# Value tiles turned by transposes, with the router's logit columns made apart, in a fused attention and mixture-of-experts kernel

## The chip, the cores and the metric

The kernel is one program on one core of a Trainium2 chip. The metric is the time of one execution in microseconds (us); "before" is the median of three runs, 772.24 us (772.15 to 772.66). The engines named below are TensorE (PE, its weight loads PEld), VectorE (DVE), ScalarE (ACT), GpSimd (POOL) and the DMA queue of SyncE (SP).

## The reference

```python
B, H, S, D = 8, 8, 576, 64                      # q, k, v: (B, H, S, D), s: (B, H, S)
scores = scale * q @ k.T + minimum(-(cum_i - cum_j), 0), causal
attn   = softmax(scores)
x      = (attn @ v) as (B*S, H*D)               # 4608 rows of 512
logits = (x / |x|) @ (emb / |emb|).T / tau      # 8 experts
e      = argmax(logits);  g = softmax(logits)[e]
out    = g * (relu(x @ w1[e]) @ w2[e])          # w1: 512 x 1024, w2: 1024 x 512
```

Since x is a product with v, a row's logits are too: with E the normed embeddings of a head (64 x 8), logits = sum over heads of attn @ (v E), up to the norm. The kernel makes v E once, as extra columns of v, and reads the logits off the attention's output.

## The kernel before

**Steps.** The attention runs in 64 steps, one for each head n of each batch (n = 8b + c8, c8 = 0 to 7); `step(n)` writes out by hand what each engine does, and each engine works its instructions off in that order. A step makes head n's scores, key-major, as two PSUM tiles (`ta_`, `tb_`, `tbl`), takes their exponentials on ACT (`expa`, `expb1`), and on POOL the part of them that bf16 loses (`pl_`, tile PL). It makes the row maxima of head n+5 from a second set of products (tiles s, spare columns of ta; PE `s1`, `sa`, `s3`, `sb`; DVE `sr`, `s3`, `sbr`), and multiplies head n-2's probabilities with its values (`pv`, 45 matmuls into om), which DVE norms into the rows xt (`norm1` to `norm3` of head n-3). The s tiles have two buffers: the third product of a step needs the first one's maximum to be read, and the fourth the second's.

**Values.** v lies head-major in memory: `vTs[b % 2]` holds for a pair of heads p (64 dimensions each on 128 partitions) 640 key columns in float32. `emm(n)` turns two or three blocks of 128 keys in step n: the block is the stationary operand, the moving one is `EN[0][:, p]`, 128 x 144: 8 logit columns of the first head, the 128 columns of the identity, 8 logit columns of the second. The result V (128 keys x 144, bank m of PSUM, which has one buffer) is scaled and split in two float16 tiles, `vh` by ACT and `vl` by DVE (`vcp`). A batch has 20 such products in its eight steps: three in even steps, two in odd ones. `loadt` and `vsq`, in steps c8 = 0 to 5, load the next batch's v and take its squares for the scale `sc` (`vscale`, c8 = 6); the vT tile of a batch is dead once its last `emm` is done.

**Rest of a batch.** When a batch's eight heads are done, the router chooses experts and scatters the rows xt to DRAM, as small DVE, PE and POOL steps between those of the next batch (`slots`, `scatter`). After step 63 the experts' matrix products follow, from about 345 us to the end.

Of the kernel before, what the change touches and what calls it, by code (L numbers as in the profile page):

```python
# [42 lines left out]
CAP = 640  # L43
# [4 lines left out]
LAST = 3  # L48
OMW = 384
XSH = 4  # L50


def fused(tc, qkh, qkc, vtin, s_in, emb, tau, w1h, w2h, out, nb=B):
# [57 lines left out]
def main(ctx, tc, qkh, qkc, vtin, s_in, emb, tau, w1h, w2h, out, shared, nb):  # L111
# [16 lines left out]
    vjunk = const.tile([128, CAP], BF16, name="vjunk")  # L128
    P32J = vjunk[:, 0:S]
    junk = const.tile([128, 1024], BF16, name="junk")  # L130
    ones = const.tile([128, 128], F32, name="ones")
    identb, tri, onesb = (const.tile([128, 128], BF16, name=n) for n in ("identb", "tri", "onesb"))
    trim = const.tile([128, 320], BF16, name="trim")
    trib = trim[:, 64:192]
# [63 lines left out]
    def heat(k):  # L198
        for _ in range(k):
            nc.tensor.matmul(om, PLs[2][:, 512:640], PLs[2][:, 0:512], start=True, stop=True)  # L200
# [74 lines left out]

    def vscale(b):
        pb = om[:, 496:500]
        nc.tensor.matmul(pb, ones, VB[b]["sq"], start=True, stop=True)
        sc = p2.tile([128, 1], F32, name="sc", bufs=3)
        si = sc.bitcast(I32)  # L280
        ws = p2.tile([128, 2], F32, name="ws", bufs=3)
        first.append(partial(nc.vector.tensor_reduce, sc, pb, AX.X, ALU.add))
        first.append(partial(soon, partial(nc.vector.tensor_scalar, sc, sc, 1.0e-30, 1.0e30, op0=ALU.max, op1=ALU.min),
                             partial(nc.vector.tensor_scalar, si, si, -0.5, float((127 + 14) * (1 << 23) + (125 << 22)), op0=ALU.mult, op1=ALU.add),
                             partial(nc.vector.tensor_single_scalar, si, si, 0x7F800000, op=ALU.bitwise_and), partial(VB[b].update, sc=sc, ws=ws),
                             partial(nc.vector.tensor_scalar, ws[:, 0:1], sc, 1.0e-6 * 2.0 ** -XSH, None, op0=ALU.mult),
                             partial(nc.vector.tensor_scalar, ws[:, 1:2].bitcast(I32), si, -1.0, float((254 + XSH) << 23), op0=ALU.mult, op1=ALU.add)))

    def emm(n):
        b, p, js = n // H, n % H // 2, ((0, 1, 2), (3, 4))[n % 2]  # L290
        t = ps_m.tile([128, 512], F32, tag="m", name="V")
        for i, j in enumerate(js):
            nc.tensor.matmul(t[:, 144 * i:144 * i + 144], vTs[b % 2][:, p, 128 * j:128 * j + 128], EN[0][:, p], start=True, stop=True)
        VB[b]["V"] = t[:, 0:144 * len(js)].rearrange("p (j c) -> p j c", c=144)

    def vcp(n, low):
        b, p, j = n // H, n % H // 2, slice(3 * (n % 2), 3 + 2 * (n % 2))
        v = VB[b]
        if "vl" not in v:
            v["vl"] = p2.tile([128, 5, H // 2, 144], F16, name="vl")  # L300
        h = v["vh"][:, j, p, 1:145]
        if not low:
            return nc.scalar.activation(h, v["V"], AF.Copy, scale=v["sc"])
        nc.vector.scalar_tensor_tensor(v["vl"][:, j, p], v["V"], v["sc"], h, op0=ALU.mult, op1=ALU.subtract)  # L304

    def hset(g):
        if g < NGg:
# [26 lines left out]
    def prep(n, k):  # L334
        g, c = n // HG, n % HG
        if n < 0:
            return
        if g == 0:
            if c == 0:
                neg(1, False, 1 - k)  # L340
            elif c < 3:
                hcopy(1, k, c - 1)
            if c < 3:
                return
        if c == 3:
            neg(g + 2, k, 0)
        elif c == 0:
            neg(g + 1, k, 1)
        else:
            hcopy(g + 1, k, c - 1)  # L350
# [136 lines left out]
    def expa(n):  # L487
        P32 = HD[n]["P32"] = P32s[n % 3]
        nc.scalar.activation(P32[:, 0:576], HD[n]["ta"][:, 256:832], AF.Exp, scale=0.125)  # L489
# [61 lines left out]
    def rsetup():  # L551
# [4 lines left out]
        def r0():  # L556
            nc.scalar.activation(P32J[0:NE, 0:DM], em, AF.Square, accum_out=a)
            nc.scalar.activation(c, a, AF.Ln, bias=tiny[0:NE])
            nc.scalar.activation(b, c, AF.Exp, scale=0.5)
# [13 lines left out]
        def r8():  # L573
            pt = ps_m.tile([128, 512], F32, tag="m", name="pe")
            for k in range(4):
                nc.tensor.transpose(out=pt[:, NE * k:NE * k + NE], in_=em[:, 128 * k:128 * k + 128], identity=ident[0:NE, 0:NE])
            pt = pt[:, 0:4 * NE].rearrange("p (c e) -> p c e", c=4)
            for i in range(2):
                v.tensor_copy(en4[64 * i:64 * i + 64, :, 136 * i:136 * i + 8], pt[64 * i:64 * i + 64])
        r0()  # L580
        r7s.append(r8)
        for f in (r1, partial(v.reciprocal, c, b), partial(v.tensor_mul, c, c, a), partial(v.tensor_add, b, b, c),
                  partial(v.tensor_scalar, b, b, 0.5, 1.0e-6, op0=ALU.mult, op1=ALU.add), partial(v.reciprocal, c, b), r7):
            f()
# [407 lines left out]
    def step(n):  # L992
# [53 lines left out]
        (sa if n > 1 else s2)(m)  # L1046
        if n < 0:
            heat(1)
        if live:
            expa(n)  # L1050
            if n != 1:
                prep(n, True)
        norm3(n - 3)
        if n == NH + 1:
            nc.sync.dma_start(zero[0:1, 0:1], XT[nb - 1][0:1, 0, 432:433])
            HT["cap"] = 24
# [92 lines left out]
            vscale(b1)  # L1149
        if live and c8 < 4:  # L1150
            loadt(b1, c8)
        if n == NH - 8:
            wissue(3)
        for _ in range(SCN[c8] if n < NH - 22 else 1 + (c8 > 5) + 4 * (n > NH - 6) if n < NH - 2 else 5 * (n >= NH)):
# [328 lines left out]
```

## Time and profile before

| | us |
|---|---|
| median of 3 runs | 772.24 |
| profiled execution | 770.33 |
| its span, first to last instruction | 768.3 |
| PE busy | 743.2 |
| ACT busy | 570.8 |
| DVE busy | 525.1 |
| POOL busy | 383.5 |

The profiled execution is 1.9 us below the median of the runs, and its span is 2.0 us shorter than its own time. PE's busy time takes a matmul as busy until its results are written; matmuls follow one another faster than that, so what one costs in a stream is read from the distance of their starts.

### The profile page before, as it was taken

What the parts mean: (1) busy time and instruction counts of PE and PEld (TensorE: products, weight loads), DVE (VectorE), ACT (ScalarE), POOL (GpSimd) and SP (SyncE); (2) the same over time, 40 slices, a digit from 0 to 9 for tenths busy, and PEclk for the clock granted to TensorE, in tenths of its full rate; (3) what the DMA queues carried; (4) which work ended last, traced back from release to release, by engine and by line L of the source; (5) the groups of instructions that cost most, each with busy time, mean ns of one, the idle gap of its engine ahead of it and who ended that gap; (6) DMA issues with size and microseconds to landing.
All of it is one profiled execution on the core that took longest, in us unless ns stands there. A gap on an engine that the chain in (4) does not pass through costs nothing. (4 is left out here: it accounts for less than half of the span.)

```text
span 768.3 us, 22128 instructions
## 1 busy us (share of the span) xinstructions
PE 743.2 (97%) x8587; PEld 550.2 (72%) x8587; DVE 525.1 (68%) x1794; ACT 570.8 (74%) x1024; POOL 383.5 (50%) x371
## 2 busy tenths in 40 slices
PE   7799999999999999999899999999999999999996
PEld 3599999999999999997464545645655555555564
DVE  7677888888888888889567666655665567645621
ACT  7789999999999999988676877738548578474410
POOL 8957798989899898774622130131221302211002
PEclk9889999999999999999999999999999999999999
DMA  8977879797979798854645965654665756643001
GB/s 157 228 175 146 173 181 206 175 216 167 211 170 214 168 206 176 209 168 156 196 150 178 185 192 168 153 194 112 166 199 114 191 168 174 210 106 88 15 15 57
DMA packets 76965, 125.46 MB, mean 163 GB/s; under 512 B 38981, under 2 KB 39385, under 8 KB 75986
## 3 DMA queue, kind: packets, MB, share of 16 engines
q0 software_dynamic: 20288, 71.07, 39.0%
q1 hardware_dynamic: 56564, 52.84, 25.6%
q8 instruction: 75, 1.23, 0.7%
q14 instruction: 38, 0.31, 0.1%
HBM read 95.38 MB, written 21.49 MB: 152 GB/s over the span
## 5 line engine op out<-in xcount | busy, mean ns | idle before, releaser
L246 POOL TENSOR_TENSOR PL<-P 128x576 f16<-128x576 f32 (+2 forms) x128 | 203.6, 1687 | 26.3 <-ACT P L489 15.5
L852 PEld LDWEIGHTS <-wt 128*128 128x128 f16 x1920 | 113.9, 98 | 87.3 <-issue 3.5
L852 PE MATMUL pxs<-xH,wt 128*128 128x512 f16 (+2 forms) x544 | 156.4, 359 | 1.8 <-PEq L901 1.0
L942 POOL DMA_INDIRECT out<-Kx,xj x39 | 41.5, 1064 | 174.6 <-DVE Kx L941 158.1
L725 POOL DMA_INDIRECT Qx<-xs,idx x41 | 42.5, 1036 | 128.1 <-ACT vjunk L807 74.6
L517 PE MATMUL om<-vh,P 128*128 128x73 f16 x945 | 105.1, 199 | 0.7 <-DVE xt L542 0.4
L518 PE MATMUL om<-vl,P 128*128 128x72 f16 x945 | 104.5, 196 | 0.0
L519 PE MATMUL om<-vh,PL 128*128 128x73 f16 x945 | 104.3, 197 | 0.0
L354 PE MATMUL s<-qkb 96*128 96x288 f32 (+4 forms) x270 | 97.0, 373 | 2.0 <-DVE M L362 1.1
L852 PE MATMUL T<-xH,wt 128*128 128x64 f16 x704 | 97.5, 193 | 0.0
L518 PEld LDWEIGHTS <-P 128*128 128x128 bf16 x960 | 94.7, 99 | 1.4 <-issue 1.0
L517 PEld LDWEIGHTS <-P 128*128 128x128 bf16 x960 | 93.6, 98 | 0.9 <-DVE vl L304 0.7
L519 PEld LDWEIGHTS <-PL 128*128 128x128 f16 x960 | 93.8, 98 | 0.0
L852 PE MATMUL pxs<-xL,wt 128*128 128x512 f16 (+1 forms) x256 | 93.0, 363 | 0.0
L362 DVE CUSTOM_DVE_ANT_0 junk<-s,mS 128x320 bf16<-128x320 f32 (+3 forms) x142 | 73.3, 524 | 5.5 <-PE s L354 3.6
L492 ACT ACTIVATE P<-tb 128x1024 f32<-128x1024 f32 x64 | 65.2, 1019 | 4.7 <-PE tb L459 3.2
L456 PE MATMUL tb<-QC,KC 128*128 128x448 f32 (+3 forms) x256 | 64.6, 311 | 0.0
L843 DVE SCALAR_TENSOR_TENSOR wt<-ring,idx,wt 128x512 f16<-128x512 f32 x80 | 56.7, 745 | 9.4 <-ACT wt L835 9.4
L452 PE MATMUL tb<-qkb 128*128 128x448 f32 (+3 forms) x256 | 61.0, 292 | 0.0
L941 DVE TENSOR_SCALAR Kx<-pxs,xj,idx 128x512 f32<-128x512 f32 x31 | 25.1, 808 | 49.9 <-PE pxs L929 38.3
L835 ACT ACTIVATE wt<-ring,idx 128x512 f16<-128x512 f32 x80 | 53.4, 711 | 7.7 <-DVE idx L822 7.7
L402 DVE CUSTOM_DVE_ANT_0 junk<-s,mS,M 128x288 bf16<-128x288 f32 x64 | 33.1, 517 | 37.0 <-PE s L354 36.3
(289 smaller groups left out, 1992.3 us busy)
## 6 DMA issues: line engine op xcount, KB each, us to landing
qkb<-qkh POOLq DMA_DIRECT2D x15, 1216.0 KB, 9.0
ring<-w2h SPq DMA_DIRECT2D x44, 256.0 KB
ring<-w1h SPq DMA_DIRECT2D x36, 256.0 KB
vT<-vtin SPq DMA_DIRECT2D x28, 320.0 KB
KC<-qkh POOLq DMA_DIRECT2D x15, 576.0 KB, 8.7
QC<-qkh POOLq DMA_DIRECT2D x15, 576.0 KB, 7.9
rw<-w1h SPq DMA_DIRECT2D x15, 256.0 KB
rw<-w2h SPq DMA_DIRECT2D x12, 256.0 KB
```

What stands on the lines that cost most here:

```text
L246: nc.gpsimd.tensor_tensor(out, a, b_, op=ALU.subtract)
L354: nc.tensor.matmul(out, G[g]["QB"][0:96, h, 128 * i:128 * i + 128], G[g]["KB"][0:96, h, lo:hi], start=True, stop=True)
L362: nc.vector.tensor_tensor_reduce(out=jk, in0=src, in1=ms, scale=1.0, scalar=NEG, op0=ALU.add, op1=ALU.max, accum_out=MP[n // 2][:, n % 2, ...
L452: nc.tensor.matmul(out, G[g]["KB"][:, h, ks:ks + 128], G[g]["QB"][:, h, 64 + qlo:64 + qhi], start=start, stop=False)
L456: nc.tensor.matmul(out, HD[n]["KC"][:, ks:ks + 128], HD[n]["QC"][:, qlo:qhi], start=False, stop=stop)
L492: nc.scalar.activation(HD[n]["P32"][:, 576:1600], HD[n]["tb"], AF.Exp, scale=0.125)
L517: nc.tensor.matmul(out, lh, vh[:, kb], start=(kb == 0), stop=False)
L518: nc.tensor.matmul(out[:, u:u + 72], lh, vl[:, kb], start=False, stop=False)
L519: nc.tensor.matmul(out, ll, vh[:, kb], start=False, stop=(kb == j))
L835: nc.scalar.activation(h, a, AF.Copy, scale=s)
L843: nc.vector.scalar_tensor_tensor(l, a, s, h, op0=ALU.mult, op1=ALU.subtract)
L852: nc.tensor.matmul(o, w[:, 128 * c:128 * c + 128], x[:, c, a:b], start=(c == 0 and k == 0), stop=(c == 3 and k == 2))
```

## The change

For batches b >= 2 (`VT0 = 2`) `emm` turns the blocks by PE transposes against the identity (128 columns), and `vcp` copies 128 columns instead of 144. The logit columns come apart, in four parts k = 0 to 3 of a batch, in the steps n = 8b - 2 to 8b + 1 (c8 = 6, 7, 0, 1). In parts 0 and 1, four matmuls, one for each pair of heads, have a 32-column stationary operand `en32[:, p]` (16 logit columns and 16 zeros) and the vT rows as moving operand (384 and 256 columns); their results go to four different quarters of the partitions of one tile L in bank m, and DVE copies L into pair 1's rows of the other, dead vT tile (`levac`). Parts 2 and 3 turn those rows by three and two transposes into L, and ACT and DVE write them to the logit columns of vh and vl (`lcp`). `r9` makes en32 on POOL in step 10. In the built program each of the four matmuls of parts 0 and 1 is two passes of weights and columns, one pair's two passes behind the other's, each on its own 32 columns of the array.

```diff
...
 LAST = 3
 OMW = 384
 XSH = 4
+VT0 = 2
 
 
 def fused(tc, qkh, qkc, vtin, s_in, emb, tau, w1h, w2h, out, nb=B):
...
     vjunk = const.tile([128, CAP], BF16, name="vjunk")
     P32J = vjunk[:, 0:S]
     junk = const.tile([128, 1024], BF16, name="junk")
-    ones = const.tile([128, 128], F32, name="ones")
+    ones = const.tile([128, 1], F32, name="ones")
+    en32 = const.tile([128, H // 2, 32], F32, name="en32")
     identb, tri, onesb = (const.tile([128, 128], BF16, name=n) for n in ("identb", "tri", "onesb"))
     trim = const.tile([128, 320], BF16, name="trim")
     trib = trim[:, 64:192]
...
 
     def vscale(b):
         pb = om[:, 496:500]
-        nc.tensor.matmul(pb, ones, VB[b]["sq"], start=True, stop=True)
+        nc.tensor.matmul(pb, ones.to_broadcast([128, 128]), VB[b]["sq"], start=True, stop=True)
         sc = p2.tile([128, 1], F32, name="sc", bufs=3)
         si = sc.bitcast(I32)
         ws = p2.tile([128, 2], F32, name="ws", bufs=3)
...
     def emm(n):
         b, p, js = n // H, n % H // 2, ((0, 1, 2), (3, 4))[n % 2]
         t = ps_m.tile([128, 512], F32, tag="m", name="V")
+        w = 144 if b < VT0 else 128
         for i, j in enumerate(js):
-            nc.tensor.matmul(t[:, 144 * i:144 * i + 144], vTs[b % 2][:, p, 128 * j:128 * j + 128], EN[0][:, p], start=True, stop=True)
-        VB[b]["V"] = t[:, 0:144 * len(js)].rearrange("p (j c) -> p j c", c=144)
-
-    def vcp(n, low):
-        b, p, j = n // H, n % H // 2, slice(3 * (n % 2), 3 + 2 * (n % 2))
+            o, v = t[:, w * i:w * i + w], vTs[b % 2][:, p, 128 * j:128 * j + 128]
+            if b < VT0:
+                nc.tensor.matmul(o, v, EN[0][:, p], start=True, stop=True)
+            else:
+                nc.tensor.transpose(out=o, in_=v, identity=ident)
+        VB[b]["V"] = t[:, 0:w * len(js)].rearrange("p (j c) -> p j c", c=w)
+
+    def vlow(b):
         v = VB[b]
         if "vl" not in v:
             v["vl"] = p2.tile([128, 5, H // 2, 144], F16, name="vl")
-        h = v["vh"][:, j, p, 1:145]
+        return v["vl"]
+
+    def vcp(n, low):
+        b, p, j = n // H, n % H // 2, slice(3 * (n % 2), 3 + 2 * (n % 2))
+        v, o = VB[b], 0 if b < VT0 else 8
+        h = v["vh"][:, j, p, 1 + o:145 - o]
         if not low:
             return nc.scalar.activation(h, v["V"], AF.Copy, scale=v["sc"])
-        nc.vector.scalar_tensor_tensor(v["vl"][:, j, p], v["V"], v["sc"], h, op0=ALU.mult, op1=ALU.subtract)
+        nc.vector.scalar_tensor_tensor(vlow(b)[:, j, p, o:144 - o], v["V"], v["sc"], h, op0=ALU.mult, op1=ALU.subtract)
+
+    LP = (slice(0, 384), slice(384, CAP))
+
+    def lpart(n):
+        k, b = (n + 2) % H, (n + 2) // H
+        return (b, k) if k < 4 and VT0 <= b < nb else (None, None)
+
+    def lmm(n):
+        b, k = lpart(n)
+        if b is None:
+            return
+        c, r = LP[k % 2], vTs[(b - 1) % 2][:, 1]
+        t = VB[b]["L"] = ps_m.tile([128, 512], F32, tag="m", name="L")[:, 0:c.stop - c.start]
+        if k < 2:
+            for p in range(4):
+                nc.tensor.matmul(t[32 * p:32 * p + 32], en32[:, p], vTs[b % 2][:, p, c], start=True, stop=True)
+        else:
+            for i in range((c.stop - c.start) // 128):
+                nc.tensor.transpose(out=t[:, 128 * i:128 * i + 128], in_=r[:, c.start + 128 * i:c.start + 128 * i + 128], identity=ident)
+
+    def levac(n):
+        b, k = lpart(n)
+        if b is not None and k < 2:
+            nc.vector.tensor_copy(vTs[(b - 1) % 2][:, 1, LP[k]], VB[b]["L"])
+
+    def lcp(n, low):
+        b, k = lpart(n)
+        if b is None:
+            return
+        v, c = VB[b], LP[k % 2]
+        if k < 2:
+            return
+        j = slice(c.start // 128, c.stop // 128)
+        x = v["L"].rearrange("p (jq c) -> p jq c", c=32)[:, :, 0:16].rearrange("p jq (i e) -> p jq i e", i=2)
+        h = v["vh"][:, j].rearrange("p j q c -> p (j q) c")
+        h = h[:, :, 1:145].rearrange("p jq (a e) -> p jq a e", e=8)[:, :, ::17]
+        if not low:
+            return nc.scalar.activation(h, x, AF.Copy, scale=v["sc"])
+        o = vlow(b)[:, j].rearrange("p j q (a e) -> p (j q) a e", e=8)[:, :, ::17]
+        for i in range(2):
+            nc.vector.scalar_tensor_tensor(o[:, :, i], x[:, :, i], v["sc"], h[:, :, i], op0=ALU.mult, op1=ALU.subtract)
 
     def hset(g):
         if g < NGg:
...
             pt = pt[:, 0:4 * NE].rearrange("p (c e) -> p c e", c=4)
             for i in range(2):
                 v.tensor_copy(en4[64 * i:64 * i + 64, :, 136 * i:136 * i + 8], pt[64 * i:64 * i + 64])
+
+        def r9():
+            nc.gpsimd.memset(en32, 0.0)
+            for i in range(2):
+                nc.gpsimd.tensor_copy(en32[64 * i:64 * i + 64, :, 8 * i:8 * i + 8], en4[64 * i:64 * i + 64, :, 136 * i:136 * i + 8])
         r0()
-        r7s.append(r8)
+        r7s.extend((r8, r9))
         for f in (r1, partial(v.reciprocal, c, b), partial(v.tensor_mul, c, c, a), partial(v.tensor_add, b, b, c),
                   partial(v.tensor_scalar, b, b, 0.5, 1.0e-6, op0=ALU.mult, op1=ALU.add), partial(v.reciprocal, c, b), r7):
             f()
...
         (sa if n > 1 else s2)(m)
         if n < 0:
             heat(1)
+        lmm(n)
         if live:
             expa(n)
+            lcp(n, False)
             if n != 1:
                 prep(n, True)
+        if live:
+            levac(n)
         norm3(n - 3)
+        if live:
+            lcp(n, True)
         if n == NH + 1:
             nc.sync.dma_start(zero[0:1, 0:1], XT[nb - 1][0:1, 0, 432:433])
             HT["cap"] = 24
...
             vscale(b1)
         if live and c8 < 4:
             loadt(b1, c8)
+        if n == 10:
+            r7s[1]()
         if n == NH - 8:
             wissue(3)
         for _ in range(SCN[c8] if n < NH - 22 else 1 + (c8 > 5) + 4 * (n > NH - 6) if n < NH - 2 else 5 * (n >= NH)):
```

The order of the instructions, in the two places that the prediction speaks of. PE in step 38 (c8 = 6), from the second of the maxima's products to the values; before:

```order
L354 MATMUL s_4282<-qkb_93 128x320
L452 MATMUL tb<-qkb_92 128x448
L452 MATMUL tb<-qkb_92 128x320
...
L459 MATMUL tb<-trim,identb 128x2x128
L293 MATMUL V<-en_185,vT_95 128x144 x3
L354 MATMUL s_4306<-qkb_93 128x288
```

and with the change:

```order
L406 MATMUL s_4361<-qkb_93 128x320
L331 MATMUL L<-vT_96,en_102 32x384 x4
L504 MATMUL tb<-qkb_92 128x448
L504 MATMUL tb<-qkb_92 128x320
...
L511 MATMUL tb<-trim,identb 128x2x128
L300 MATMUL V<-ident,vT_95 128x128 x3
L406 MATMUL s_4391<-qkb_93 128x288
```

The four products of part 0 stand ahead of the tb products; the three products with 144 columns have become three transposes. DVE in step 40 (c8 = 0), from the first maximum of the step to the third product's; before:

```order
L362 ISA junk,M<-s_4485,mS 128x448
L362 ISA M 128x1
L534 RECIPROCAL z<-z 128x5
L542 TENSOR_TENSOR xt<-om,z 128x5x72
L362 ISA junk,M<-s_4494,mS 128x320
L362 ISA M 128x1
L399 TENSOR_REDUCE M_4378<-s_4505 128x1
```

and with the change:

```order
L414 ISA junk,M<-s_4576,mS 128x448
L414 ISA M 128x1
L586 RECIPROCAL z<-z 128x5
L594 TENSOR_TENSOR xt<-om,z 128x5x72
L356 SCALAR_TENSOR_TENSOR vl<-L,sc,vh_108 128x12x8 x2
L414 ISA junk,M<-s_4585,mS 128x320
L414 ISA M 128x1
L451 TENSOR_REDUCE M_4463<-s_4604 128x1
```

The two writes of logit columns stand between the norming of the rows and the second maximum; in steps of c8 = 6 and 7 the copy of L stands one place higher, ahead of the norming.

## Rows read from the trace of the kernel before

**Rows 1.** The page, whole span: busy time and share; PE's granted clock in tenths.

```profile
PE 743.2 (97%) x8587; PEld 550.2 (72%) x8587; DVE 525.1 (68%) x1794; ACT 570.8 (74%) x1024; POOL 383.5 (50%) x371
...
PEclk9889999999999999999999999999999999999999
```

**Rows 2.** Busy time in windows: steps 32, 35, 37, 38, 39 and the sum of 32 to 39.

```profile
core 0: us, PE busy (x) PEld busy (x) DVE busy (x) ACT busy (x) POOL busy (x), PEclk, DMA share, GB/s
189.53:194.44 4.91, 4.91 (x78) 4.86 (x74) 3.92 (x19) 4.29 (x6) 4.47 (x4) 1.00 1.10 238
...
204.16:209.28 5.12, 5.06 (x77) 4.71 (x74) 4.66 (x19) 5.05 (x8) 4.01 (x4) 1.00 0.63 196
...
214.20:219.33 5.13, 5.13 (x87) 5.06 (x83) 4.07 (x19) 5.06 (x8) 5.13 (x5) 1.00 1.06 207
219.33:224.59 5.26, 5.26 (x79) 5.04 (x76) 4.49 (x20) 5.21 (x8) 4.76 (x5) 1.00 0.81 209
224.59:229.36 4.77, 4.77 (x74) 4.71 (x73) 3.80 (x18) 3.92 (x6) 4.59 (x5) 1.00 0.18 67
sum 39.83, PE 39.77 PEld 38.84 DVE 32.66 ACT 36.94 POOL 35.01; mean PE 4.97 PEld 4.85 DVE 4.08 ACT 4.62 POOL 4.38
```

**Rows 3.** Waits by engine and line, window of steps 32 to 39: us in total, times, longest.

```profile
PEld s L354 <- DVE M L362: 0.6, 2, 0.4
```

**Rows 4.** PE in order of time, step 40: start, us.

```profile
229.36 0.27 PE L459 MATMUL ta<-trim,identb 128*128 128x256 bf16 x1
...
230.35 0.52 PE L452 MATMUL tb<-qkb 128*128 128x448 f32 x2
...
231.73 0.90 PE L293 MATMUL V<-en,vT 128*128 128x144 f32 x6
232.38 0.39 PE L354 MATMUL s<-qkb 96*128 96x288 f32 x1
```

**Rows 5.** What writes or reads tile V: duration ns least, median, most.

```profile
L293 PE MATMUL V<-en,vT x320: 286/286/577, 32.9 to 344.1; 128*128 128x144 f32 x160
```

**Rows 6.** PE in order of time, from 344.0 us: transposes of float32 blocks.

```profile
344.22 1.04 PE L758 MATMUL pxs<-ident,Qx 128*128 128x128 f32 x8
```

**Rows 7.** PE in order of time, from 18.3 us: matmuls on eight rows amid whole ones.

```profile
18.44 0.60 PE L200 MATMUL om<-PL 128*128 128x512 f16 x2
18.97 0.41 PE L576 MATMUL pe<-ident,em 8*128 8x8 f32 x4
19.31 0.47 PE L354 MATMUL s<-qkb 96*128 96x448 f32 x1
```

**Rows 8.** Groups by line and shape: busy us, mean ns of one.

```profile
L758 PE MATMUL pxs<-ident,Qx 128*128 128x128 f32 x16 | 2.3, 274 | 0.1
L304 DVE SCALAR_TENSOR_TENSOR vl<-V,sc,vh 128x432 f16<-128x432 f32 x32 | 21.2, 663 | 2.3 <-ACT vh L303 2.3
L304 DVE SCALAR_TENSOR_TENSOR vl<-V,sc,vh 128x288 f16<-128x288 f32 x32 | 16.0, 499 | 0.6 <-ACT vh L303 0.6
L634 DVE TENSOR_TENSOR om<-om,oh 128x40 f32<-128x40 f32 x8 | 1.6, 206 | 0.2
L567 DVE COPY en<-ident 128x512 f32<-128x512 f32 x1 | 0.5, 492 | 0.9 <-POOL ident masks.py:199 0.9
L303 ACT ACTIVATE vh<-V,sc 128x432 f16<-128x432 f32 x32 | 19.8, 618 | 0.0
L303 ACT ACTIVATE vh<-V,sc 128x288 f16<-128x288 f32 x32 | 15.9, 498 | 0.3 <-PE V L293 0.3
```

**Rows 9.** DVE in order of time, step 40.

```profile
230.79 0.53 DVE L542 TENSOR_TENSOR xt<-om,z 128x360 f32<-128x360 f32 x1
231.24 0.48 DVE L362 CUSTOM_DVE_ANT_0 junk<-s,mS 128x320 bf16<-128x320 f32 x1
...
232.80 0.52 DVE L402 CUSTOM_DVE_ANT_0 junk<-s,mS,M 128x288 bf16<-128x288 f32 x1 [0.70 <-PE s L354]
```

**Rows 10.** ACT in order of time, step 40.

```profile
230.46 0.65 ACT L489 ACTIVATE P<-ta 128x576 f32<-128x576 f32 x1 [0.58 <-PE ta L456]
```

## The prediction

> **What bounds the kernel now.** I read the page first: PE is busy 743 of 768 us [rows 1], so PE's queue is the first suspect, and its clock is at the full level (2.4 GHz) outside the start; the clock plays no part. The change lies in the attention's 64 steps, so the next view is busy time by step in a settled batch, steps 32 to 39 [rows 2]: 39.83 us, PE 39.77, ACT 36.94, POOL 35.01, DVE 32.66. The reader is to see that PE has no room, that ACT has 2.9 us, and that ACT's room is not everywhere: in steps 35, 37 and 38 it is busy 5.05 of 5.12, 5.06 of 5.13 and 5.21 of 5.26 us. Then the waits: in these eight steps PE waits only twice, 0.6 us together, the longer 0.4, the other 0.2 (the third product of a step, for the first maximum) [rows 3]. So almost any change of PE's stream shows in the time, and a DVE or ACT that comes late shows as a wait of PE.
>
> **What a value product costs, and a transpose.** PE's starts in step 40 [rows 4]: six matmul records for three products. Each lasts 0.286 us alone [rows 5], the six last 0.90, so five starts lie in 0.90 - 0.286 = 0.614 us: 0.123 us a pass, two passes a product, 0.246. A pass of 144 columns thus takes 0.123/144 = 0.85 ns a column. Eight float32 transposes of 128 columns take 1.04 us [rows 6], one record each of 0.274 [rows 8]: (1.04 - 0.274)/7 = 0.110, and one pass only. A product that becomes a transpose saves 0.136 us; 20 of them in a batch save 2.72. They are all on PE's path.
>
> **What is added to PE.** Five transposes of logit rows a batch: 5 x 0.110 = 0.55. The eight column-tiled products: by the price a column, one pass takes 384 x 0.85 = 0.328 us in part 0 and 256 x 0.85 = 0.219 in part 1, and a group is four matmuls of two passes. No row shows matmuls on different columns of the array beside each other, so this is bounded from both sides: all eight passes of a group one behind the other, 8 x (0.328 + 0.219) = 4.38 us a batch; all four matmuls beside each other, 2 x 0.547 = 1.09. I take the lower end, since the four have their own columns, weights and output partitions and no data in common, and keep the upper one for the range. Entering and leaving such a group: the nearest rows are four matmuls on eight rows of the array amid whole ones [rows 7]. The last 512-column matmul before starts about 18.66 (18.44 + 0.60 - 0.38) and streams some 0.22 us; the first small one starts at 18.97, 0.09 later than it could. I take 0.09 for each of the two ways in and two ways out, 0.36 a batch; the bounds are nothing and double that.
>
> **What is added to DVE and ACT, and what hides it.** DVE: two copies of 384 and 256 columns (a 512-column copy takes 0.49 [rows 8], so at most that and about 0.3), four small writes of 96 or 64 numbers (between the 0.21 of 40 numbers and the 0.50 of 288 [rows 8]; I take 0.25), less 16 columns a block of vl: (0.663 - 0.499)/144 = 1.1 ns a column, 0.05 or 0.04 on each of eight, 0.36. Net some 1.4 us a batch, against 7.2 idle. But the place counts. In step 40 a second maximum starts at 231.24, lasts 0.48, and the fourth product at 232.38 needs it: about 0.65 us of room [rows 4, 9]. With the change, PE turns three blocks between 230.35 and 230.68, results at 230.95; ACT, whose exponential ends at 231.11 [rows 10], writes the high logits (192 numbers at 0.83 ns each from its two shapes [rows 8], 0.42) until about 231.5; DVE, waiting since 231.24 and with the norm, maxima and sums queued behind, writes the low ones until about 232.05, and the maximum ends near 232.5. PE reaches the fourth product at 232.38 + 0.33 - 3 x 0.136 = 232.30: a wait of 0.2. The step after has the same chain, one transpose less, and saves two products, not three: about as much. In steps of c8 = 6 and 7 the copy waits for L too, with the same DVE work behind it, but PE has tb, third product and values, 1.7 us, between L and the fourth product; DVE has copy, norm and maximum, some 1.5. No wait there, and the 0.2 that PE waits in step 38 for the first maximum falls beside L. So +0.4 - 0.2 = +0.2; the bounds are -0.2 (small writes as quick as the 40-number row) and +0.8.
>
> ACT gains 0.79 us of logit writes and loses 8 x 0.03. In steps 35 to 38, where it has no room, PE's part shrinks by 0.27 or 0.41 a step and ACT's by 0.03: ACT falls some 0.8 us behind by the end of step 37 and makes it good beside L. PE feels that only through vh, vl and the next first maximum; I allow 0.1 us a batch. POOL makes en32 once, in step 10, beside its idle time (4.8 us of 39.8). The load of pair 1 of v now waits on SP for the logit transposes of c8 = 1; the maxima's rows are sent behind it. The transposes are over 1.4 us into that step, so this costs nothing unless PE is late.
>
> **The sum.** A batch: -2.72 + 0.55 + 1.09 + 0.36 + 0.2 + 0.1 = -0.42 us; six batches (2 to 7), -2.5. On the profiled execution's 770.33 that is 767.8; the median is 1.9 higher, so I forecast 772.24 - 2.5 = 769.7. The last batch has no squares on ACT and may gain somewhat more; the experts' products after it are untouched. Case range: without entry cost and waits, -1.08 a batch, 765.8; with both at their upper bounds, +0.5, 775; most of it 766 to 771.5.
>
> **Rivals.**
> *The passes keep their order (slower).* In the built program the two passes of one product stand together: first pass of pair 0, second of pair 0, first of pair 1. The second of a pair needs the columns that the first still streams through. If PE holds back all that stands behind a pass that can't start, only the second pass of a pair and the first of the next lie beside each other: five passes in a row instead of two. Price: 5 x 0.547 = 2.74 instead of 1.09, +1.65 a batch, so +1.23 a batch and +7.4 in all; less what ACT and DVE no longer wait for (0.1), 779. It decides as soon as a group lasts longer than 2 + 0.42/0.547 = 2.8 passes. For it: in all rows of the trace PE's starts are in the program's order, and one product's two passes are 0.123 apart, never closer [rows 4, 5]. Against: a matmul's start may stand ahead of the end of the one before (232.38 is 0.25 before the last V pass ends), so PE takes more than one in hand. The Trainium skill (TensorE: Matmul & The Clock Gate, Part 3: Packing small matmuls) says that matmuls start and end strictly in program order; by that sentence pair 1's first pass can't end before pair 0's second, which is this rival. The same section gives 2.38 times for three column tiles with one matmul each, which speaks for overlap as such; no row here shows either.
> *No overlap at all.* Eight passes in a row: +3.29 a batch against the forecast, +2.87 net, +17: 789. For it: nothing in this trace ever overlaps two streams. Against: the separate columns.
> *ACT becomes the bound.* If steps 35 to 38 can't be shorter than ACT's work, what three of them save on values (0.27 + 0.41 + 0.27 = 0.95) is lost, net +0.4 a batch: 774.5. For it: ACT's 5.05 of 5.12 [rows 2]. Against: PE nowhere waits for ACT there, and ACT has 2.9 us to catch up in the other steps.
>
> **Chances.** Forecast 0.46, passes in order 0.34, no overlap 0.12, ACT the bound 0.08. What a measurement here can tell from no change is about 0.2%, 1.5 us: faster means below 770.7. The forecast gives that in five of six cases (0.38; with a little from the others 0.40); within 0.2%: 0.06 of the forecast, 0.04 of ACT's case and 0.02 else, 0.12; slower 0.48, nearly all from the two rivals on the passes. The single likeliest case is thus a gain, though a loss has the larger sum. The range must hold forecast, ACT's case and most of the first rival: 766 to 780.5; the likeliest case's own is 766 to 771.5.
>
> **What would show it.** The eight records of a part-0 group: from the first start to the next tb product 0.75 us (two passes and the switches), 1.7 (five) or 2.7 (eight). V transposes 0.110 apart. Steps of c8 = 2 to 5 shorter by 0.27 to 0.41 each; steps of c8 = 6 and 7 longer by about 0.3. DVE's second maximum in c8 = 0 and 1 named as what PE's fourth product waits for, 0.2 each. ACT without idle from c8 = 3 to 6, and no PE wait on it. I am wrong if a part-0 group is longer than 1.1 us (2.8 passes and the switches), if steps of c8 = 3 to 5 stay above 4.9 us, or if PE gets gaps over 0.5 us a step.

## The result and the profile after

The changed kernel takes 777.35 us (median of 6 runs, 775.68 to 777.85), the kernel before 772.36 beside it: 1.0062 times, 95% interval 1.0049 to 1.0075, so 0.6% slower. Run again on another chip: 777.03 against 774.07, 1.0040 [1.0024, 1.0055]. The forecast was 769.7, a small gain; a small loss came. The range, 766 to 780.5, holds the result, but its upper end stood for a case that did not come (five passes a group), so that is luck. The profiled execution of after took 775.68 us with a span of 773.7.

The page of after, to compare with [rows 1]: PE and ACT have a little more work, DVE 9 us more.

```profile
PE 745.4 (96%) x8593; PEld 540.1 (70%) x8593; DVE 533.9 (69%) x1830; ACT 573.6 (74%) x1036; POOL 384.5 (50%) x374
...
PEclk9989999999999999999999999999999999999999
```

The windows of steps 32 to 39 of after, all but step 36, answering [rows 2]; a step goes from one start of ta on PE to the next.

```profile
191.89:196.93 5.04, 5.04 (x77) 4.83 (x74) 4.43 (x21) 4.50 (x7) 4.13 (x4) 1.00 1.07 232
196.93:201.98 5.05, 5.05 (x77) 4.75 (x75) 4.47 (x21) 4.78 (x7) 4.88 (x5) 1.00 0.98 210
201.98:206.49 4.51, 4.51 (x75) 4.46 (x72) 3.45 (x16) 3.98 (x6) 4.45 (x6) 1.00 1.10 225
206.49:211.84 5.35, 5.05 (x75) 4.48 (x72) 4.91 (x19) 5.32 (x8) 4.32 (x4) 1.00 0.63 185
...
216.35:221.15 4.80, 4.80 (x84) 4.73 (x81) 3.97 (x18) 4.73 (x7) 4.80 (x5) 1.00 0.98 191
221.15:226.84 5.69, 5.69 (x84) 4.85 (x82) 5.09 (x21) 5.64 (x9) 5.18 (x5) 1.00 0.87 205
226.84:232.09 5.25, 5.25 (x80) 4.62 (x80) 4.10 (x19) 4.01 (x6) 5.08 (x6) 1.00 0.20 74
sum 40.20, PE 39.90 PEld 37.19 DVE 34.39 ACT 37.42 POOL 35.02; mean PE 4.99 PEld 4.65 DVE 4.30 ACT 4.68 POOL 4.38
```

A settled batch is 40.20 us instead of 39.83: +0.37 where -0.42 was forecast. By step (c8 = 0 to 7) it went from 4.91 4.80 4.91 5.12 4.92 5.13 5.26 4.77 to 5.04 5.05 4.51 5.35 4.51 4.80 5.69 5.25. The reader is to see two things: c8 = 2, 4 and 5 became as short as forecast, and c8 = 3, which should have gone to 4.85, became longer; it is the one step here in which PE is idle (5.05 of 5.35). Steps c8 = 6 and 7 grew by 0.43 and 0.48, where about 0.3 was named. The waits of PE's weight loads in the same stretch, answering [rows 3]:

```profile
PEld tb L504 <- issue: 1.0, 2, 0.6
PEld s L406 <- DVE M L414: 0.8, 2, 0.6
PEld L L331 <- PE ta L508: 0.3, 2, 0.2
```

The first and the last are new and stand behind and ahead of the two tiled groups; the middle one is the wait for a maximum, now up to 0.6 (0.4 before).

**A tiled group.** PE in order of time in step 38 of after (c8 = 6, part 0):

```profile
222.00 0.31 PE L406 MATMUL s<-qkb 96*128 96x320 f32 x1
222.24 0.85 PE L331 MATMUL L<-vT,en 128*32 128x384 f32 x8
223.02 0.62 PE L504 MATMUL tb<-qkb 128*128 128x448 f32 x2
223.48 0.51 PE L508 MATMUL tb<-QC,KC 128*128 128x448 f32 x2
...
224.50 0.49 PE L300 MATMUL V<-ident,vT 128*128 128x128 f32 x3
224.75 0.38 PE L406 MATMUL s<-qkb 96*128 96x288 f32 x1
```

and tile L on PE in two narrow windows (up to 222.40 and up to 222.62):

```profile
L331 PE MATMUL L<-vT,en x4: 510/510/510, 222.2 to 222.3; 128*32 128x384 f32 x4
...
L331 PE MATMUL L<-vT,en x8: 486/498/510, 222.2 to 222.6; 128*32 128x384 f32 x8
```

Four records start together at 222.24, the other four at about 222.59, one pass later: two passes, all four tiles side by side. (The rows don't say which pair a record belongs to. But wherever one float32 product has the whole array, its two passes start one pass apart, 0.33 us for these 384 columns in the run with one whole product below; so the four that start together are of four pairs.) From start to the next tb product there are 0.78 us; 0.75 was forecast for this case, 1.7 and 2.7 for the rivals. But the group also costs ahead and behind: from the s product to the group 0.24 us, where s to tb was 0.15 before, and the tb product behind it 0.46 to the next start instead of 0.36. That is 0.97 us of PE's time for part 0, and by the same differences 0.75 for part 1. The three transposes of V take 0.25 to the next product, where three products took 0.65 [rows 4].

The weight loads in the same places:

```profile
222.24 0.16 PEld L331 LDWEIGHTS L<-vT,en 128*32 128x32 f32 x8 [0.16 <-PE ta L508]
223.02 0.19 PEld L504 LDWEIGHTS tb<-qkb 128*128 128x128 f32 x1 [0.62 <-issue]
```

The group's first load and the first load behind it start within 2 ns of their products, 222.240 and 223.023: no load runs ahead there.

**Step 35 (c8 = 3).** Before, DVE's vl and PE's third product:

```profile
203.81 0.66 DVE L304 SCALAR_TENSOR_TENSOR vl<-V,sc,vh 128x432 f16<-128x432 f32 x1
```

```profile
206.08 0.40 PE L354 MATMUL s<-qkb 96*128 96x288 f32 x1
```

After, PE in order of time:

```profile
207.86 0.51 PE L508 MATMUL tb<-QC,KC 128*128 128x448 f32 x2
208.67 0.40 PE L406 MATMUL s<-qkb 96*128 96x288 f32 x1 [0.30 <-DVE M L414]
```

DVE in order of time:

```profile
206.47 0.62 DVE L315 SCALAR_TENSOR_TENSOR vl<-V,sc,vh 128x384 f16<-128x384 f32 x1 [0.24 <-ACT vh L314]
207.00 0.77 DVE L79 TENSOR_REDUCE om<-xt 128x40 f32<-128x320 f32 x1
...
207.99 0.61 DVE L414 CUSTOM_DVE_ANT_0 junk<-s,mS 128x448 bf16<-128x448 f32 x1
```

The third product starts 0.81 us after the tb product ahead of it; where nothing is late it is 0.35, and in this step before it was 0.56 (205.52 to 206.08). It waits for the first maximum (207.99 to 208.6), that for a reduction of 0.77 us and two small operations, these for vl, and vl waits 0.24 for ACT's vh. The step starts at 206.49, so vl starts when the step does; before, it started at 203.81 in a step that began at 204.16, 0.35 earlier. ACT had not become slower: vh follows two exponentials and a copy that hang on the step's start. In step 34 it starts 3.88 us behind that start (205.86) as it did before (203.11, 3.87), but the step was cut from 4.91 to 4.51.

ACT's exponentials of ta in steps 34 and 39 show how full that engine is:

```profile
203.08 0.65 ACT L541 ACTIVATE P<-ta 128x576 f32<-128x576 f32 x1 [0.48 <-PE ta L508]
...
227.94 0.65 ACT L541 ACTIVATE P<-ta 128x576 f32<-128x576 f32 x1 [0.63 <-PE ta L508]
```

Between the two ACT pauses for no more than 0.03 us until the 0.63 at the end: 24.2 us of work in a row. Counted from the step's start, this exponential comes at 1.10 in step 34, 1.60 in step 35, 1.79 in step 38 and 1.10 again in step 39. A lag that begins in step 34 can be made good in step 39 only.

**Step 32 (c8 = 0).** DVE in order of time, from the low logits on:

```profile
194.03 0.54 DVE L356 SCALAR_TENSOR_TENSOR vl<-L,sc,vh 128x96 f16<-128x96 f32 x2 [0.21 <-ACT vh L353]
194.49 0.48 DVE L414 CUSTOM_DVE_ANT_0 junk<-s,mS 128x320 bf16<-128x320 f32 x1
```

PE in order of time:

```profile
192.89 0.49 PE L334 MATMUL L<-ident,vT 128*128 128x128 f32 x3
193.14 0.59 PE L504 MATMUL tb<-qkb 128*128 128x448 f32 x2
...
194.46 0.29 PE L511 MATMUL tb<-trim,identb 128*128 128x256 bf16 x1
194.72 0.52 PE L300 MATMUL V<-ident,vT 128*128 128x128 f32 x3
195.04 0.40 PE L406 MATMUL s<-qkb 96*128 96x288 f32 x1
```

The low logits end 2.68 us after the step's start and the second maximum 3.08 after it; the working in the prediction gave 2.69 and 3.14. The fourth product waits 0.07 for it. But V waits too, some 0.14: its bank m holds L until the low logits have been read (194.57), and V starts at 194.72.

### The profile page after: what moved, and what is told of

It is laid out like the page before. It is cut to its first block, busy times and chain, and to the rows that moved or that the text cites. A ratio compares the mean times of both kernels' runs of the same rounds, so it can differ in the third digit from the quotient of the medians.

```text
span 773.7 us, 22216 instructions
## 1 busy us (share of the span) xinstructions
PE 745.4 (96%) x8593; PEld 540.1 (70%) x8593; DVE 533.9 (69%) x1830; ACT 573.6 (74%) x1036; POOL 384.5 (50%) x374
## 5 line engine op out<-in xcount | busy, mean ns | idle before, releaser
L504 PE MATMUL tb<-qkb 128*128 128x448 f32 (+3 forms) x256 | 62.9, 299 | 0.0
L998 DVE TENSOR_SCALAR Kx<-pxs,xj,idx 128x512 f32<-128x512 f32 x31 | 25.1, 809 | 49.2 <-PE pxs L986 37.5
L406 PEld LDWEIGHTS s<-qkb 96*128 96x128 f32 x270 | 51.2, 191 | 9.8 <-DVE M L414 6.2
```

The lines of the kernel that those rows point to most:

```text
L406: nc.tensor.matmul(out, G[g]["QB"][0:96, h, 128 * i:128 * i + 128], G[g]["KB"][0:96, h, lo:hi], start=True, stop=True)
L504: nc.tensor.matmul(out, G[g]["KB"][:, h, ks:ks + 128], G[g]["QB"][:, h, 64 + qlo:64 + qhi], start=start, stop=False)
```

## Experiments

The later runs were on other chips; each time stands against runs of the kernel before beside it. Lengths of steps and batches are differences of starts on PE, as above.

**Transposes alone.** The logit columns are left out from batch 2 on, and with them the groups, logit transposes, copies and small writes; vl keeps the tile of two batches before. Routing is then different, so only the attention's steps are read.

```diff
-            v["vl"] = p2.tile([128, 5, H // 2, 144], F16, name="vl")
+            v["vl"] = p2.tile([128, 5, H // 2, 144], F16, name="vl") if b < VT0 else VB[b - 2]["vl"]
...
     def lpart(n):
         k, b = (n + 2) % H, (n + 2) // H
-        return (b, k) if k < 4 and VT0 <= b < nb else (None, None)
+        return None, None
```

> Batches 3 to 8 turned by transposes, the logit columns left out (those of batches 1 and 2 stay in their place, so experts are chosen wrongly and only the attention's steps count). Before, a settled batch took 39.83 us; changed, 40.20. Theory (a step's ACT chain exponential, copy, exponential, vh is tied to the step's start, so a shorter PE step leaves DVE's vl and what is queued behind it later in the next step): the 2.72 us of the values are not all had; in c8 = 3 PE's wait for the first maximum stays near 0.7 us, a batch takes 37.5 to 37.9. Rival (only the tiled groups cost more than I priced): 37.1, and the wait in c8 = 3 stays at 0.3.

Steps 34, 35 and 38 of a settled batch, and the sum over eight:

```profile
194.94:199.45 4.51, 4.51 (x75) 4.46 (x71) 3.51 (x16) 4.21 (x6) 4.45 (x6) 1.00 1.10 247
199.45:204.80 5.35, 5.05 (x75) 4.48 (x73) 4.91 (x19) 5.33 (x8) 5.34 (x6) 1.00 0.82 213
...
214.11:219.50 5.39, 5.16 (x76) 4.71 (x74) 4.45 (x20) 5.34 (x9) 4.90 (x5) 1.00 0.98 218
...
sum 38.11, PE 37.58 PEld 36.23 DVE 32.59 ACT 36.59 POOL 35.06; mean PE 4.70 PEld 4.53 DVE 4.07 ACT 4.57 POOL 4.38
```

38.11, 1.72 less than before, where PE's own saving is 2.7, and somewhat above the theory's 37.5 to 37.9. Step c8 = 3 is 5.35 here too, with the same wait of vl:

```profile
199.43 0.62 DVE L315 SCALAR_TENSOR_TENSOR vl<-V,sc,vh 128x384 f16<-128x384 f32 x1 [0.24 <-ACT vh L314]
```

So this loss belongs to the shorter steps, not to the logits. About one microsecond a batch of the saving is lost, in c8 = 3 and in c8 = 6 (5.39 where 4.85 was to come). In c8 = 6 the same chain is seen: vl waits 0.35 for vh and starts 0.17 behind the step's start, where before it started 0.26 ahead of it. From ACT's exponential of step 34 to that of step 39 it is 24.57 us, of which ACT works 24.2; before, it was 25.35. So ACT's queue had room for 1.1 of the 1.77 that PE saves in these five steps: some 0.65 of the lost microsecond lies in ACT's work, whatever the order on DVE.

**Logits on top.** All the logit work, with value products of 144 columns kept.

```diff
-        w = 144 if b < VT0 else 128
+        w = 144
...
-            if b < VT0:
+            if b < B:
                 nc.tensor.matmul(o, v, EN[0][:, p], start=True, stop=True)
...
-        v, o = VB[b], 0 if b < VT0 else 8
+        v, o = VB[b], 0
```

> The products of 144 columns are kept, and all of the new logit work is done beside them (it writes the same values again). Groups as in the changed trace 0.97 and 0.75, transposes 0.58, no vl delay since PE's steps aren't shorter: a batch about 42.1 (2.3 more than before), in all +12 to +14, 785 to 786 us. If the tiled groups also disturbed others (DVE's copy, waits of 0.3 each in c8 = 0 and 1), 42.7 and 788. If the priced groups of the prediction were right, 41.8 and 784.

787.16 us, 1.0166 [1.0138, 1.0194]; a batch 42.35, +2.5, between the theory's 42.1 and the 42.7 of its second case. The forecast's terms for the additions (0.55 + 1.09 + 0.36 + 0.2) make 2.2; the 0.3 more stands in the two steps with groups (6.09 and 5.54 against 5.26 and 4.77). Step c8 = 3 is what it was before:

```profile
212.10:217.22 5.12, 5.07 (x77) 4.70 (x73) 4.67 (x19) 5.05 (x8) 3.75 (x4) 1.00 0.43 113
```

With all of the logit work and no shorter steps, the loss of c8 = 3 is not there.

**High part of V ahead of the second exponential, on ACT.**

```diff
-            expb1(n)
-            if n:
-                vcp(n, False)
+            if n >= 16:
+                vcp(n, False)
+            expb1(n)
+            if 0 < n < 16:
+                vcp(n, False)
```

> The changed kernel, from batch 3 on with ACT's vh written ahead of the second exponential. Theory (vl waits for vh behind that exponential): DVE's 0.2 to 0.3 wait before vl goes, PE's wait in c8 = 3 falls from 0.46 + 0.21 to about 0.4, a batch from 40.2 to 39.8, in all -2 us, 775. Rival (only the groups' price): no change, 777.3. If ACT's second exponential is needed sooner than I think (POOL's PL), slower, 779.

774.86 us, 1.0007 [0.9995, 1.0018]; batches of 39.93 to 40.13. Step c8 = 3 is 5.05 to 5.08, and vl starts without a wait, 0.34 ahead of the step's start (206.44):

```profile
206.10 0.61 DVE L315 SCALAR_TENSOR_TENSOR vl<-V,sc,vh 128x384 f16<-128x384 f32 x1
```

The chain from ACT's vh to PE's third product is shown by this: one order changed on ACT, vl is back where it stood before the change, and PE waits 0.3 less in that one step. The 0.2 that the third product waited there before the change stays.

**The reduction of 0.77 us moved out of the chain.** It goes into step c8 = 2, behind the third product's reduction.

```diff
             sb(m)
+            if live and c8 == 2 and n > 16:
+                slot()
             sbr(m)
```

> The changed kernel, with the router's 0.8 us sum over the logit columns moved on DVE from ahead of the first maximum of c8 = 3 into DVE's idle time ahead of the fourth product's maximum of c8 = 2. Theory: PE's waits in c8 = 3 (0.7 us, of which 0.3 stood before the change too) go, of which 0.1 may come back in c8 = 2: a batch 39.5, in all -4 us, 773.5. Rival (only the groups' price): the 0.3 that was there before goes, 775.5.

777.08 us, 1.0028 [1.0012, 1.0044]; the batch only fell to 40.08. Step c8 = 3 went from 5.35 to 4.53, but c8 = 2 rose to 4.81 (PE's value products start 0.3 later; by the profile they wait for the moved reduction itself), and c8 = 5 from 4.80 to 5.10, where the wait for vh came back, longer:

```profile
215.82 0.62 DVE L315 SCALAR_TENSOR_TENSOR vl<-V,sc,vh 128x384 f16<-128x384 f32 x1 [0.53 <-ACT vh L314]
```

ACT's lag was not removed, only passed on: the wait in c8 = 3 had also given ACT time. The expected 39.5 was missed because I had counted one wait and not the next.

**Second maximum first on DVE.** In the changed kernel it goes ahead of the copy of L, the low logits and the norm; the low logits go ahead of the norm as well.

```diff
+        if n >= 16:
+            sr(m, 2)
         if live:
             levac(n)
+            lcp(n, True)
         norm3(n - 3)
-        if live:
-            lcp(n, True)
...
-        sr(m, 2)
+        if n < 16:
+            sr(m, 2)
```

> The changed kernel, with the second row maximum ahead of the copy of the transposed logits, the low part of the logit copy and the normalisation on VectorE, from batch 1 on. Theory (TensorE's fourth product waits in steps 0 and 1 of a batch, and in step 3 the value operations wait, because the second maximum is queued behind those three): these waits of about 0.07, 0.18 and 0.21 us go, while the third product's wait in step 3 stays (0.8 against 0.35 unhindered, it hangs on ScalarE's high part of V); a batch 39.7 to 39.9 us instead of 40.20, 774 to 776 us. Rival (VectorE's order does not matter, these waits are all ScalarE's): 40.2 a batch, as the changed kernel.

775.86 us, 1.0020 [1.0005, 1.0034]; batches of 39.93 to 39.99. Steps 0 and 1 fell to 4.99 and 4.87, step 3 to 5.11 (its third product still starts 0.81 after tb, the wait of 0.21 ahead of the fourth is gone), and step 5 rose by 0.2. The theory holds for each wait; the batch came out a little above its range.

**Both orders.** The two edits together.

> The changed kernel with two orders altered: the second row maximum first on VectorE, as in the run beside it, and on ScalarE the high part of V ahead of the second exponential. Theory (two separate chains, both felt in step 3): step 3 falls from 5.35 to about 4.75, a batch to 39.4 to 39.6 us, and the time to 771 to 773 us, a little below the kernel before on the same chip. Rival (the waits only move, as when the exponential sum was moved): step 3 falls but steps 5 and 6 rise, a batch stays at about 40.0 and the time within 0.2% of, or above, the kernel before.

773.21 us, 0.9994 [0.9981, 1.0006]: no different from the kernel before. Steps 35 and 38, and the sum of the batch:

```profile
205.28:210.11 4.83, 4.81 (x74) 4.44 (x72) 4.48 (x19) 4.81 (x8) 3.76 (x5) 1.00 0.64 198
...
219.43:225.35 5.92, 5.85 (x85) 4.90 (x82) 4.92 (x21) 5.87 (x9) 5.33 (x5) 1.00 0.89 194
...
sum 39.70, PE 39.61 PEld 37.15 DVE 33.52 ACT 37.37 POOL 35.12; mean PE 4.95 PEld 4.64 DVE 4.19 ACT 4.67 POOL 4.39
```

Step 3 came to 4.83, where the prediction had 4.85, and step 6 rose by 0.23, where ACT is busy 5.87 of 5.92. So part of the theory (39.4 to 39.6) and part of its rival: 39.70, 0.13 below before. The five steps from 34 on still take 24.57 us, with 24.2 of ACT's work.

**The same orders in the kernel before**, first the second maximum alone, then both.

> The kernel before with the second row maximum ahead of the normalisation on VectorE and nothing else. Theory (in the kernel before that maximum was in time: no wait of TensorE hangs on it in steps 32 to 39 but the 0.4 us in step 35): 39.6 to 39.85 a batch, within 0.2% of the kernel before. Rival (the gain of that order belongs to it and not to the changed kernel): 39.4 a batch or less, faster by 0.3%.

> The kernel before with both orders altered: second row maximum ahead of the normalisation, and the high part of V ahead of the second exponential. Theory (the waits of step 3 of 0.4 and 0.2 us in the kernel before are the same two chains): step 3 from 5.12 to about 4.9, which is the length that TensorE's own work has there, a batch about 39.4, faster by about 0.2 to 0.3%. Rival (ScalarE's order was right for the kernel before and its second exponential then comes late): 39.8 or more.

The first: 773.61 us, 0.9997 [0.9982, 1.0012], batches of 39.83 to 39.90, as expected. The second: 774.92, 1.0020 [1.0003, 1.0037], and my theory of it fell: step c8 = 3 stayed at 5.13. Step 35 starts at 207.13 there, and DVE reads

```profile
206.78 0.66 DVE L304 SCALAR_TENSOR_TENSOR vl<-V,sc,vh 128x432 f16<-128x432 f32 x1
207.36 0.81 DVE L78 TENSOR_REDUCE om<-xt 128x40 f32<-128x320 f32 x1
```

vl stands 0.35 ahead of the step, as in the kernel before: it never waited for vh there. What PE waits 0.2 for in that step of the kernel before is DVE's own queue, the 0.81 us reduction; the second wait of [rows 3], 0.2 on the weight load, is not in this step but in step 38. The same step thus had one cause of waiting before the change and two after it.

**The group as one whole product**, to measure what tiling costs beside its passes. The four weight blocks stand side by side and multiply one pair's rows, so the logits are other values, and only the attention's steps are read.

```diff
-            for p in range(4):
-                nc.tensor.matmul(t[32 * p:32 * p + 32], en32[:, p], vTs[b % 2][:, p, c], start=True, stop=True)
+            nc.tensor.matmul(t, en32.rearrange("p q c -> p (q c)"), vTs[b % 2][:, 0, c], start=True, stop=True)
```

> Each group of four column-tiled products is one product on the whole array with all four weight blocks side by side, for one of the four row pairs alone (the logits are other values, so the work behind the attention is not comparable; read the attention's steps). Theory (a group pays about 0.31 us for changing into and out of the tiled form, beside its two passes of 0.85 ns a column): without the tiles the extra of TensorE in the steps of the two products falls from 0.97 and 0.75 to about 0.66 and 0.44 us, steps 6 and 7 of a batch to 5.38 and 4.94. Rival (the fixed part belongs to any float32 product between half-precision ones, not to the tiles): it stays, 5.69 and 5.25.

PE in order of time, step 38:

```profile
221.27 0.81 PE L330 MATMUL L<-vT,en 128*128 128x384 f32 x2
221.62 0.81 PE L503 MATMUL tb<-qkb 128*128 128x448 f32 x2
222.26 0.51 PE L507 MATMUL tb<-QC,KC 128*128 128x448 f32 x2
```

Its weight loads:

```profile
221.12 0.34 PEld L330 LDWEIGHTS L<-vT,en 128*128 128x128 f32 x2
```

From the product's start to the second tb product there are 0.99 us; tb alone takes 0.36, so the product costs 0.64, two passes of 384 columns at 0.83 ns a column. Part 1, by the same differences, costs 0.42. The tiled groups cost 0.97 and 0.75: 0.33 us more in both, whatever the columns. The theory holds on the price. The first weight load starts 0.15 us ahead of its product here (221.12 and 221.27), with the tiled group only 2 ns ahead; that the load is what the 0.33 us consists of is likely but not shown. Step 39 fell by 0.29 to 4.96; step 38 fell only to 5.60, since the second maximum, behind the copy of L, is then late for PE's shorter step.

**Two tiles of 64 columns** instead of four of 32 (other pairs than needed).

```diff
-            for p in range(4):
-                nc.tensor.matmul(t[32 * p:32 * p + 32], en32[:, p], vTs[b % 2][:, p, c], start=True, stop=True)
+            for p in range(2):
+                nc.tensor.matmul(t[64 * p:64 * p + 64], en32[:, 2 * p:2 * p + 2].rearrange("p q c -> p (q c)"),
+                                 vTs[b % 2][:, p, c], start=True, stop=True)
```

> Each group has two tiles of 64 columns instead of four of 32 (again for other row pairs than needed, so only the attention's steps count). Theory (the fixed part is the change of form, once in and once out): steps 6 and 7 stay at 5.69 and 5.25. Rival (it is a price for each tile, some 0.08 us, by its weight load): two tiles save 0.15 us a group, 5.54 and 5.10. A second rival (the passes of four tiles only partly overlap): a like fall.

Steps 38 and 39 are 5.70 and 5.26, unchanged. The two tiles' records last about as long as the four tiles' did (379 to 510 ns):

```profile
L331 PE MATMUL L<-vT,en x48: 379/458/537, 101.4 to 309.9; 128*64 128x384 f32 x24, 128*64 128x256 f32 x24
```

The 0.33 us is a price of the change of form, not of the tiles, and the third and fourth tile cost nothing.

**Both kernels again**, for waits of PE that no row explained.

> The changed kernel once more. Theory: settled batches of 40.20 us again and the same ratio, 1.005 to 1.0075; the 0.62 us more in step 13 and the 2.0 us wait in step 61 of the first profile do not both come back at the same place, since they are no part of the change. Rival (they belong to the changed kernel): step 13 at 5.75 and step 61 at 6.07 again.

> The kernel before once more, for the waits of TensorE that no row explains. Theory (such waits fall in the last batches of any of these kernels, with the execution): a wait of over 1 us between 325 and 355 us, or the same few of 0.7 to 0.9 us as in its first profile, and settled batches of 39.83 us. Rival (only the changed kernels have the long ones): none over 1 us there.

After: 777.03 us, 1.0040 [1.0024, 1.0055], a little below the expected ratio, with settled batches of 40.21 to 40.23. Its step 13 is 5.12, so the 0.62 us in the first profile was of that execution. Step 61 is 5.49 (6.07 in the first profile). Before: one run, 775.57 us, batches of 39.82 to 39.93, and step 61 is 5.76, 4.67 in its first profile. One line of its waits, 324 to 345 us:

```profile
PE om L517 <- DVE idx L819: 1.4, 1, 1.4
```

So the long wait near the attention's end comes with the kernel before as well. What sets it is open; it isn't the change.

## Why the prediction was wrong, step by step

**Right.** *The saving:* V's blocks take 0.65 to 0.25 and 0.40 to 0.14 us; with somewhat quicker products behind them that is 2.76 a batch on PE, 2.72 forecast. *The logit transposes:* 0.52 (0.55). *The passes:* two a group. The rival "passes keep their order", with a chance of 0.34, and "no overlap" both fall with the eight records of the group. By the Trainium skill (TensorE: Matmul & The Clock Gate, Part 3: Packing small matmuls) matmuls start and end strictly in program order. This trace does not bear it out for float32 products on column tiles: in the built program, as the section on the change has it, pair 0's two passes stand ahead of pair 1's, but the first passes of all four pairs start within 0.02 us, the second passes 0.35 later. The same section gives 2.38 times for three column tiles. Here, with four, eight passes one behind the other would be 8 x 0.32 = 2.55 us for part 0, an estimate from the price a column, against 0.97 measured: 2.6 times.

*ACT's lag:* some 0.8 us by the end of step 37, made good beside L. Its exponential of ta comes 0.7 later in step 38 than before (1.79 us behind the step's start, 1.12 before) and is in place again in step 39.

**Mis-sized.** *Entering and leaving a group:* 0.18 taken, bounds nothing to 0.36, measured 0.33; with the passes as they came, +0.27 a batch. The row I went by [rows 7] was of a few matmuls on eight rows of the array, another form. *DVE in c8 = 0 and 1:* a wait of the fourth product of 0.07 and 0.18 (0.2 each); the waits of V for bank m, 0.14 and 0.10, were not in the sum, so it is 0.1 more than forecast. The 0.2 in step 38 went, as forecast.

**Failed.** "PE feels that only through vh, vl and the next first maximum; I allow 0.1 us a batch." The lag and its path were right, the price was not: its place was not looked up. In c8 = 3 DVE has a 0.77 us reduction between vl and the first maximum, and there PE's third product was already 0.2 late before the change (0.56 behind the tb product instead of 0.35), so a later vl has no room at all. vl came 0.33 later in relation to the step, and the first maximum with it: the third product waits 0.46 instead of 0.21, and the second maximum, later too, makes the fourth product wait 0.21. Step c8 = 3 became 5.35 instead of 4.85, +0.5 a batch against the 0.1 allowed. Transposes alone show it without any logit work, the logits on top do not show it without the shorter steps, and the altered order on ACT takes 0.3 of it away, both orders all of it (4.83).

The sum a batch, in the terms of the prediction: -2.76 + 0.52 + 1.72 (the two groups, 0.97 + 0.75) + 0.87 (waits of 1.32 in place of 0.45) = +0.35, against the measured +0.37. A wait counts here with what it costs behind it: a third product that was late has 0.24 us to the next start instead of 0.13. Where the forecast had -2.72 + 0.55 + 1.45 + 0.3, the group prices bring +0.27 and the waits nearly +0.6.

The rival "ACT becomes the bound" (0.08, 774.5) was the nearest, and in part it is what happened. Its price, 0.95 a batch of the saving lost, is what transposes alone lose (1.0), with ACT at work without a pause from step 34 to step 38. It had the loss in steps 35 to 37; in fact 36 and 37 became as short as PE's work (4.51 and 4.80), and ACT was felt through DVE, in step 35 and, without the groups, in step 38. In the changed kernel PE's group lies in step 38, and no product of that step waits. Of the three signs named for being wrong, one came plainly: a step of c8 = 3 to 5 above 4.9. A second, gaps of PE over 0.5 us in a step, came in that same step if its two waits are added (0.67).

**From the batch to the whole.** Five settled batches at +0.37 make 1.8 us; steps 14 and 15, which have batch 2's groups and no saving yet, add 1.6 (6.09 and 5.53 for 5.27 and 4.78), and steps 56 to 62 of the last batch, without step 61, give back 0.5 (26.9 for 27.4 in both pairs of profiles): 2.9 us, near the 3.0 between the medians on the second chip. Step 61 itself went from 4.67 to 6.07 in the first profiles and from 5.76 to 5.49 in the repeats, so no part of it can be put down to the change. On the first chip the medians differ by 5.0; the rest of that lies in parts where two profiles of the same kernel differ by as much, and is not settled.

## What to carry to other kernels

Where one engine is full, shortening its step does not only take away its work: the other engines' results, tied to the step's start, come later against the step's end, so look for the step in which the next engine's queue has its longest extra operation, and price the wait there, not over the batch. A wait that is moved away from such a step can come back in the next one, as long as the lag behind it stays; so add up the second engine's work over the whole stretch in which it never pauses, here 24.2 us in five steps, before counting on a saving of the first. And for a form of instruction that no row shows, the cost of changing into it belongs in the range with more than the nearest other form gives.

## What the runs showed of the hardware that was not expected

Four float32 products on four column tiles run as two passes in all: the first passes start 6 to 7 ns apart, the second ones the same way one pass later (222.240 to 222.260 and 222.587 to 222.607 us in the changed kernel). Between whole-array products such a group pays 0.33 us beside its passes, the same for 384 and 256 columns (0.97 against 0.64, 0.75 against 0.42), and for two tiles and four; a float32 product of the same columns on the whole array, in the same place, pays nothing (0.64 us for two passes of 384 columns). The weight load of the group, and that of the product behind it, start 2 ns ahead of their products, the whole-array product's 0.15 us ahead.
